# Two of three transposed K waves loaded as 16 rows of 131,072 columns, with score weights read at a step of 256 or 64 bytes

## The chip, the cores and the metric

The kernel runs on one core of one Trainium2 chip. The metric is the device time of one execution in microseconds (us). A short name is used throughout: TensorE is the matmul engine, and every matmul on it has its stationary operand, the weights, loaded by a weight load with its own record in the trace (PEld; the kernel before has 12,376 records of each). ScalarE (ACT), VectorE (DVE) and GpSimd (POOL) do the rest, and one queue on SyncE (SP) issues nearly all DMA (q1 of the page before: 291.99 of 294.14 MB).

Each set of experiments ran on one chip, with its own runs of the kernel before. Those runs had medians of 1054.96, 1054.72 and 1054.58 us for the three sets, so the sets can be compared to about half a microsecond.

## The reference, cut to what matters

There are two independent attention layers, A and B, of the same size. Each has 16 batches, 144 queries, 16 heads, 512 keys and a head width of 256, all in bf16.

```python
q = (x @ wq).reshape(16, 144, 16, 256).transpose(0, 2, 1, 3)
scores = einsum("bhqd,bhkd->bhqk", q, k_cache) * 256 ** -0.5
p = softmax(scores, axis=-1)
o = einsum("bhqk,bhkd->bhqd", p, v_cache)
out = o.transpose(0, 2, 1, 3).reshape(16, 144, 4096) @ wo
```

K and V of one head are 262 KB each, and there are 512 heads to go through (2 layers, 16 batches, 16 heads). One such head is called a unit. Several experiments below read wrong weights on purpose, and they passed all the same. Their times count, their results don't.

## The kernel before

The score matmuls of this kernel take K with the head width on the partitions (`kt_sb`), so K is transposed first. Units 0 to 47 have it done by TensorE. From unit 48 on, 29 "waves" of 16 units come in by a transposing DMA, into a ring of two waves. Every wave is one DMA of 4.19 MB:

```python
KW, KR = 16, 32                       # units in a wave, units in the ring
kt_sb = sb("kt_sb", [128, 8, KR * 128], BF16)
...
def t_load_k(W):
    ...
    src = ks[pr].rearrange("b h (p c) d -> (b h p) (c d)", c=4)[r0 * 128:(r0 + n) * 128, :]
    def e(q):
        return q.dma_start_transpose(kt_sb[:, :, c0:c0 + n * 128], src).then_inc(sems[sem], 16)
```

The source is read as 2048 rows of 1024 columns. After the transpose, the 128 weights of one score matmul lie next to each other in a partition. V comes by plain DMA, two units at a time, with one run of 2 KiB for each partition and unit. A key's place must agree between K and V: partition p holds keys 4p to 4p+3, as four chunks c.

```python
def v_source(t, G):
    ...
    return t[pr][b, h0:h0 + UV].rearrange("u (p c) d -> p u (c d)", p=128)

def t_s(U):                           # scores of one unit: 8 matmuls
    for k in range(2):
        for c in (2 * k, 2 * k + 1):
            for dc in range(2):
                t.matmul(s_ps[bank][:, (c % 2) * SQ:(c % 2 + 1) * SQ],
                         lhsT=kt_sb[:, 2 * c + dc, ko:ko + 128],
                         rhs=qt_sb[:, qsl, dc, :], start=(dc == 0), stop=(dc == 1))
        ...                           # exp on ScalarE into pt_sb
```

Besides these there are the query projection, the product with V (8 matmuls a unit), the sums of the exponentials on GpSimd, VectorE and TensorE, and the output projection. All of it is laid out ahead of time by a planner in the program. The planner issues each DMA by its own estimate of when the data is needed and of how long the queue is held; for a K wave of n units the estimate is `2.0 + 0.97 * n` us.

## Time and profile before

| | before |
|---|---|
| time, median of 2 runs | 1054.01 us (1053.67 to 1054.36) |
| span of the profiled run | 1051.6 us, mean granted clock 0.996 |
| TensorE busy | 1029.9 us, 98% |
| next busiest engine | ACT, 794.1 us, 76% |
| eight score matmuls, start to start of the next group | 0.50 us |
| time in which TensorE waited for a K wave | 6.9 us |

Two resources are near their end: TensorE, busy for 98% of the span, and the DMA queue, whose row of the forty slices stands at 9 up to the last two. The prediction below shows the lines for both. Two more rows of the page, from the list of the costliest groups, are wanted later. They are the score matmuls and their weight loads; the two numbers after the first bar are the busy time in us and the mean length of one record in ns, and behind the last bar stands the idle time of the engine before them with what ended most of it.

```profile
L1112 PE MATMUL s_ps<-qt_sb,kt_sb 128*128 128x144 bf16 x4096 | 341.3, 227 | 8.0 <-DMA kt_sb<-in_B_k_cache_dram 6.9
...
L1112 PEld LDWEIGHTS s_ps<-qt_sb,kt_sb 128*128 128x128 bf16 x4096 | 288.3, 98 | 60.0 <-issue 7.3
```

The mean records are 227 and 98 ns long, but one score matmul follows another after 62.5 ns. The records of successive matmuls thus overlap: each is 3.6 times as long as the distance to the next. What a matmul costs has to be read from start to start. And this is the DMA total of the page, with packets by size:

```profile
DMA packets 591748, 294.14 MB, mean 280 GB/s; under 512 B 502592, under 2 KB 516768, under 8 KB 591584
```

### The profile page before, as it was taken

How to read it: one execution, taken by the hardware profiler on the slowest of the kernel's cores; microseconds unless marked ns; L12 is line 12 of the kernel's file. 1: busy time of each engine (PE TensorE's matmuls, PEld its weight loads, DVE VectorE, ACT ScalarE, POOL GpSimd, SP SyncE). 2: the span in 40 equal slices, each digit the busy share in tenths (PEclk: the TensorE clock that was granted, in tenths of full speed). 3: DMA queues.
4: the chain of work that ended last, by engine and by line, in shares of the span. 5: the costliest groups of instructions: out<-in, count | busy, mean ns of one | idle time of the engine just before them, and what ended most of it. 6: DMA issues, size and time to landing. Idle time of an engine off the chain costs nothing.

```text
span 1051.6 us, 32329 instructions
## 1 busy us (share of the span) xinstructions
PE 1029.9 (98%) x12376; PEld 875.8 (83%) x12376; DVE 737.7 (70%) x2039; ACT 794.1 (76%) x2365; POOL 636.2 (61%) x1030
## 2 busy tenths in 40 slices
PE   7999999999999999999999799999999999999998
PEld 6999888888888888888888688888888888888885
DVE  5776676777776776676777567677776667777775
ACT  5877677777777787777877567787877777788785
POOL 3555556666666666666756456566666666666673
PEclk9999999999999999999999999999999999999999
DMA  9999999999999999999999999999999999999950
GB/s 291 363 341 340 263 306 266 288 288 293 290 300 284 285 237 257 302 290 297 265 288 340 268 276 300 295 272 300 282 269 269 299 258 305 302 271 257 289 187 14
DMA packets 591748, 294.14 MB, mean 280 GB/s; under 512 B 502592, under 2 KB 516768, under 8 KB 591584
## 3 DMA queue, kind: packets, MB, share of 16 engines
q1 hardware_dynamic: 591584, 291.99, 110.1%
q8 instruction: 99, 1.62, 0.6%
q14 instruction: 65, 0.53, 0.2%
HBM read 161.48 MB, written 4.13 MB: 157 GB/s over the span
## 4 chain that ended last, share of the span: by engine, by line
PE 90%; DMA 6%; SPq 1%; ACT 1%; DVE 1%; issue 0%; POOL 0%; ACTq 0%; DVEq 0%
PE s_ps L1112 23%; PE ot_ps L1168 23%; PE qp_ps L1081 22%; PE op_ps L1284 19%; DMA kt_sb<-in_B_k_cache_dram 2%; DMA kt_sb<-in_A_k_cache_dram 2%; PE ot_ps L1184 2%; DMA wq_sb<-in_A_wq_dram 1%; PE qp_ps L1032 1%; PE s_ps L1032 1%; PE qp_ps L1284 1%; ACT rinv_sb L1205 1%; DMA v_sb<-in_B_v_cache_dram 0%; SPq L1002 0%; ACT pt_sb L1122 0%
## 5 line engine op out<-in xcount | busy, mean ns | idle before, releaser
L1132 POOL TENSOR_TENSOR pp_sb<-pt_sb 128x288 f32<-128x288 bf16 x512 | 384.6, 751 | 320.1 <-ACT pt_sb L1122 305.4
L1122 ACT ACTIVATE pt_sb<-s_ps 128x288 bf16<-128x288 f32 x1024 | 364.6, 408 | 182.7 <-PE s_ps L1112 176.5
L1220 DVE TENSOR_TENSOR ring<-ot_ps,rinv_sb 128x288 bf16<-128x288 f32 (+2 forms) x640 | 241.8, 394 | 159.4 <-ACT rinv_sb L1205 155.0
L1112 PE MATMUL s_ps<-qt_sb,kt_sb 128*128 128x144 bf16 x4096 | 341.3, 227 | 8.0 <-DMA kt_sb<-in_B_k_cache_dram 6.9
L1168 PE MATMUL ot_ps<-pt_sb,v_sb 128*128 128x144 bf16 x4096 | 340.2, 226 | 0.3 <-DMA v_sb<-in_A_v_cache_dram 0.2
L1112 PEld LDWEIGHTS s_ps<-qt_sb,kt_sb 128*128 128x128 bf16 x4096 | 288.3, 98 | 60.0 <-issue 7.3
L1205 ACT ACTIVATE rinv_sb<-ln_sb 64x144 f32<-64x144 f32 x928 | 298.3, 321 | 24.2
L1081 PE MATMUL qp_ps<-xt_sb,wq_sb 128*128 128x288 bf16 (+1 forms) x2368 | 302.3, 271 | 2.2 <-DMA wq_sb<-in_A_wq_dram 1.2
L1284 PE MATMUL op_ps<-wo_sb,ring 128*128 128x448 bf16 x1120 | 285.5, 352 | 0.0
L1081 PEld LDWEIGHTS qp_ps<-xt_sb,wq_sb 128*128 128x128 bf16 x2368 | 212.7, 98 | 77.1 <-DVE qt_sb L1094 2.3
L1168 PEld LDWEIGHTS ot_ps<-pt_sb,v_sb 128*128 128x128 bf16 x4096 | 274.3, 98 | 1.2 <-DMA v_sb<-in_A_v_cache_dram 0.4
L1137 POOL TENSOR_TENSOR p_sb<-pp_sb 128x144 f32<-128x144 f32 x464 | 227.4, 490 | 74.2 <-DVE ps_sb L1146 9.4
L1235 DVE TENSOR_REDUCE run_sb<-ot_ps 128x1 bf16<-128x144 f32 x560 | 146.5, 304 | 76.7 <-ACT ln_sb L1192 42.6
L1146 DVE TENSOR_TENSOR ps_sb<-p_sb 64x144 bf16<-64x144 f32 x464 | 156.1, 336 | 45.8 <-POOL p_sb L1137 32.5
L1095 DVE CAST qt_sb<-qp_ps 128x576 bf16<-128x576 f32 x216 | 162.1, 750 | 14.0 <-PE qp_ps L1081 10.9
L1284 PEld LDWEIGHTS op_ps<-wo_sb,ring 128*128 128x128 bf16 x1120 | 93.7, 98 | 20.1
L1192 ACT ACTIVATE ln_sb<-ot_ps 128x144 f32<-128x144 f32 x232 | 67.9, 293 | 32.3 <-PE ot_ps L1184 24.5
L1184 PE MATMUL ot_ps<-ps_sb,ones 128*128 128x144 bf16 x280 | 63.3, 226 | 0.0
L1094 DVE CAST qt_sb<-qp_ps 128x288 bf16<-128x288 f32 x80 | 35.8, 447 | 2.8 <-PE qp_ps L1081 2.6
L1040 ACT ACTIVATE kt_sb<-qp_ps 128x512 bf16<-128x512 bf16 x48 | 28.9, 603 | 6.1 <-PE qp_ps L1032 6.1
L1137 POOL TENSOR_TENSOR ps_sb<-pp_sb 128x144 bf16<-128x144 f32 x48 | 23.5, 490 | 6.9 <-PE ot_ps L1184 0.3
L1184 PEld LDWEIGHTS ot_ps<-ps_sb,ones 128*128 128x128 bf16 x280 | 27.4, 98 | 0.0
(29 smaller groups left out, 154.5 us busy)
## 6 DMA issues: line engine op xcount, KB each, us to landing
v_sb<-in_A_v_cache_dram SPq DMA_DIRECT2D x128, 512.0 KB, 6.9
v_sb<-in_B_v_cache_dram SPq DMA_DIRECT2D x128, 512.0 KB, 7.0
v_sb<-in_A_k_cache_dram SPq DMA_DIRECT2D x22, 512.0 KB, 9.9
out_dram<-ost_sb SPq DMA_DIRECT2D x36, 112.0 KB, 6.1
wo_sb<-in_A_wo_dram SPq DMA_DIRECT2D x8, 448.0 KB, 8.5
wo_sb<-in_B_wo_dram SPq DMA_DIRECT2D x8, 448.0 KB, 8.7
wq_sb<-in_B_wq_dram SPq DMA_DIRECT2D x4, 768.0 KB, 9.3
wq_sb<-in_A_wq_dram SPq DMA_DIRECT2D x3, 768.0 KB, 9.2
```

The source lines that it names most:

```text
L1081: ins = t.matmul(acc, lhsT=wq_sb[:, kc, c0:c0 + 128], rhs=xt_sb[:, kc, xo:xe + 1:max(xe - xo, 1), :], start=(kc == 0), stop=(kc == 3))
L1095: return v.tensor_copy(qt_sb[:, a:b + 1:b - a, :, :], qp_ps[:, :, 0:2 * SQ].rearrange("p e (u q) -> p u e q", u=2))
L1112: ins = t.matmul(s_ps[bank][:, (c % 2) * SQ:(c % 2 + 1) * SQ], lhsT=kt_sb[:, 2 * c + dc, ko:ko + 128], rhs=qt_sb[:, qsl, dc, :], start=(dc ...
L1122: return a.activation(pt_sb[:, psl, 2 * k:2 * k + 2, :].rearrange("p b q -> p (b q)"), s_ps[bank][:, 0:2 * SQ], AF.Exp, scale=DH ** -0.5)
L1132: return g.tensor_tensor(pp_sb[:, :, :], pt_sb[:, psl, 0:2, :], pt_sb[:, psl, 2:4, :], op=ALU.add)
L1137: return g.tensor_tensor(dst, pp_sb[:, 0, :], pp_sb[:, 1, :], op=ALU.add)
L1146: return v.tensor_tensor(ps_sb[p0:p0 + 64, sl, :], p2_sb[0:64, :], p2_sb[64:128, :], op=ALU.add)
L1168: ins = t.matmul(ot_ps[ob][:, dc * SQ:(dc + 1) * SQ], lhsT=v_sb[:, vsl, j, c * DH + dc * 128:c * DH + (dc + 1) * 128], rhs=pt_sb[:, sl, c, ...
L1205: return a.activation(rinv_sb[p0:p0 + 64, sl, :], ln_sb[h0:h0 + 64, :], AF.Exp, scale=-1.0)
L1220: ins = v.tensor_tensor(ring[:, 2 * h:2 * h + 2, r0:r0 + q1 - q0], ot_ps[ob][:, 0:2 * SQ].rearrange("p (c q) -> p c q", c=2)[:, :, q0:q1], ...
L1235: return v.tensor_reduce(run_sb[:, k, j:j + 1], ot_ps[ob][:, 2 * SQ:3 * SQ], axis=AX.X, op=op)
L1284: ins = t.matmul(acc[0:m, 0:D], lhsT=ring[:, c, col0:col0 + m], rhs=wo_sb[:, c, :], start=(c == op_first), stop=(c == op_last))
```

## The change

The intent is to load K in longer rows. Of every three waves one stays as it was (form 0). In the other two the source is read as 16 rows, one for each head, of 131,072 columns, so that each row is 256 KiB in one piece. The price is that the transposed data lies otherwise in the ring: element k of head u is followed by element k of head u+1. The 128 weights of one matmul are then no longer neighbours.

- Form 1 keeps the key order 4p + c. It reads every 128th element, a step of 256 bytes.
- Form 2 takes the key order 128c + p. It reads every 32nd element, a step of 64 bytes. V has to follow that order, so its runs shrink from 2 KiB to 512 bytes.

```diff
-        kt_sb = sb("kt_sb", [128, 8, KR * 128], BF16)
+        kt_sb = sb("kt_sb", [128, KR // KW, KW * 1024], BF16)
...
             src = ks[pr].rearrange("b h (p c) d -> (b h p) (c d)", c=4)[r0 * 128:(r0 + n) * 128, :]
+            if k_form(u0):
+                src = ks[pr].rearrange("b h k d -> (b h) (k d)")[r0:r0 + n, :]
...
+                dst = kt_sb[:, u0 % KR // KW, :]
+                if k_form(u0):
+                    dst = dst.rearrange("p (k u) -> p k u", u=KW)
+                else:
+                    dst = dst.rearrange("p (c n) -> p c n", c=8)
+                return q.dma_start_transpose(dst, src).then_inc(sems[sem], 16)
...
+        def k_form(U):
+            return 0 if U < P0 else U // KW % 3
+
+        def k_weights(U, c, dc):
+            ring = kt_sb[:, U % KR // KW, :]
+            f = k_form(U)
+            if f == 0:
+                return ring.rearrange("p (c n) -> p c n", c=8)[:, 2 * c + dc, U % KW * 128:U % KW * 128 + 128]
+            ring = ring.rearrange("p (k e u) -> p k e u", u=KW, e=2)[:, :, dc, U % KW]
+            return ring[:, c::4] if f == 1 else ring[:, c * 128:(c + 1) * 128]
...
+            if k_form(UV * G) == 2:
+                return t[pr][b, h0:h0 + UV].rearrange("u (c p) d -> p u c d", p=128)
...
-                                           lhsT=kt_sb[:, 2 * c + dc, ko:ko + 128],
+                                           lhsT=k_weights(U, c, dc),
```

Left out are the V destination with the same dimensions and the same ring indexing in the copy of TensorE's transposes. No instruction is added on any engine, and their order stays.

More of the change, by code (lines that the diff above doesn't have):

```diff
@@ L985, in t_load_k @@
             src = ks[pr].rearrange("b h (p c) d -> (b h p) (c d)", c=4)[r0 * 128:(r0 + n) * 128, :]
+            if k_form(u0):
+                src = ks[pr].rearrange("b h k d -> (b h) (k d)")[r0:r0 + n, :]
             def e(q):
-                return q.dma_start_transpose(kt_sb[:, :, c0:c0 + n * 128], src).then_inc(sems[sem], 16)
-            S.add(SP, e, writes=[(("kt", u % KR), u) for u in range(u0, u1)], dma_sem=sem, name="k%d.%d" % (W, n))
+                dst = kt_sb[:, u0 % KR // KW, :]
[4 more added lines that the diff above has]
+                return q.dma_start_transpose(dst, src).then_inc(sems[sem], 16)
+            S.add(SP, e, writes=[(("kt", u % KR), u) for u in range(u0, u1)], dma_sem=sem, name="k%d.%d" % (W, n))
+        def k_form(U):
[7 more added lines that the diff above has]
+            return ring[:, c::4] if f == 1 else ring[:, c * 128:(c + 1) * 128]
         def v_source(t, G):
@@ L1001, in e @@
             def e(q):
-                return q.dma_start(v_sb[:, sl, :, :], src).then_inc(sems["v%d" % sl], 16)
+                dst = v_sb[:, sl, :, :]
+                if k_form(UV * G) == 2:
+                    dst = dst.rearrange("p u (c d) -> p u c d", c=4)
+                return q.dma_start(dst, src).then_inc(sems["v%d" % sl], 16)
             S.add(SP, e, writes=[(("v", sl), ("v", G))], dma_sem="v%d" % sl, name="v%d" % G)
@@ L1037, in ev @@
             def ev(g):
-                dst = kt_sb[:, 4 * k:4 * k + 4, ko:ko + 128]
+                dst = kt_sb[:, U % KR // KW, :].rearrange("p (c n) -> p c n", c=8)[:, 4 * k:4 * k + 4, U % KW * 128:U % KW * 128 + 128]
                 src = tr_ps[k][:, 0:512].rearrange("p (c q) -> p c q", c=4)
```

## The prediction

> **What bounds the kernel now.** I read first the page's busy shares and its forty slices, then the groups by cost, then the order of matmuls, the weight loads of the score line, the DMA queue in order of time, and last the stretches between.
>
> ```profile
> PE 1029.9 (98%) x12376; PEld 875.8 (83%) x12376; DVE 737.7 (70%) x2039; ACT 794.1 (76%) x2365; POOL 636.2 (61%) x1030
> ...
> DMA  9999999999999999999999999999999999999950
> ...
> PE s_ps L1112 <- DMA kt_sb<-in_B_k_cache_dram: 6.9, 1, 6.9
> ```
>
> TensorE is busy for 1029.9 of 1051.6 us, so all of its idle time is 21.7 us: about 6 in the first 10 us, 5.6 in the last 32, and 6.9 in one wait for a K wave (third line, from the list of waits; it is the only one that counts). No other engine is over 76%. The DMA row, though, is as full as TensorE's. So there are two resources near their end. Which of them has how much room decides the case.
>
> TensorE first. A matmul's record overlaps its neighbours', so I take start to start from the order of time:
>
> ```profile
> 20.42 0.39 PE L1032 MATMUL s_ps<-qt_sb,v_sb 128*128 128x128 bf16 x4
> 20.64 0.66 PE L1081 MATMUL qp_ps<-xt_sb,wq_sb 128*128 128x144 bf16 x8
> 21.14 0.66 PE L1112 MATMUL s_ps<-qt_sb,kt_sb 128*128 128x144 bf16 x8
> 21.64 0.39 PE L1032 MATMUL qp_ps<-qt_sb,v_sb 128*128 128x128 bf16 x4
> ```
>
> Eight score matmuls take 21.64 - 21.14 = 0.50 us, 62.5 ns each; four transposes with 128 moving columns take 0.22 us, 55 ns each. Each of these has its own weight load, all from adjacent columns. So a contiguous load needs at most 55 ns and lies wholly beside the matmul before it. Nothing in this trace loads weights with a step, so the disputed cost isn't there to be read. What is there is one clue:
>
> ```profile
> L1112 PEld LDWEIGHTS s_ps<-qt_sb,kt_sb x16: 95/98/98, 300.1 to 301.7; 128*128 128x128 bf16 x16
> ...
> L1112 PEld LDWEIGHTS s_ps<-qt_sb,kt_sb x8: 104/147/147, 602.0 to 602.7; 128*128 128x128 bf16 x8
> ```
>
> (min/median/max ns of two windows.) Right after the 6.9 us wait TensorE runs slow: eight score matmuls begin within 0.91 us, not 0.50, and the load's record grows by 49 ns. If the clock halved there, as 0.91/0.50 suggests, the part that scales with the clock is about 49 ns at full speed[...]. I rest on this with care, since the page says that ends are modelled.
>
> DMA second.
>
> ```profile
> 245.17 19.03 SPq L988 DMA_TRANSPOSE kt_sb<-in_A_k_cache_dram  x1
> 264.24 0.58 SPq L1313 DMA_DIRECT2D out_dram<-ost_sb  x1
> 264.87 7.16 SPq L1002 DMA_DIRECT2D v_sb<-in_A_v_cache_dram  x7
> ...
> 248.00:263.00 15.00, 15.00 (x176) 12.47 (x174) 10.76 (x29) 11.18 (x35) 9.78 (x16) 1.00 1.30 226
> 267.00:273.00 6.00, 6.00 (x75) 5.07 (x73) 3.81 (x10) 4.75 (x15) 3.59 (x6) 1.00 1.01 385
> ```
>
> A wave of 16 heads is one transpose of 4.19 MB. It holds the queue for 19 us and runs at 226 GB/s (last column of the windows), where plain V loads run at 385. K waves are issued 30 to 31 us apart here (214.6, 245.2): 19 for K, 8 V loads of 0.52 MB at 385 GB/s are 11 more. The queue is nearly full, but TensorE still sets the pace.
>
> [...]
>
> **The change, part by part.** Waves begin at unit 48, so there are 29; those with number 4, 7, ... 31 (10) take the 256-byte step, 5, 8, ... 29 (9) the 64-byte step, and 10 stay. 19 waves x 16 units x 8 = 2432 of 4096 score matmuls get stepped weights. The order of instructions on every engine is the old one; no matmul, exponential or sum is added. The ring has the same size, and 16 units are freed at the same place.
>
> K transposes: 19 move the same 4.19 MB from 16 contiguous rows of 256 KiB instead of 2048 rows of 2 KiB. [...] This is work beside TensorE: it relieves the queue and shortens nothing, except that the wave waited for at 602 us (still an old one, but behind two new ones in the queue) arrives earlier. That returns 6.9 us and the slow-clock stretch behind it, about 2 us: -9.
>
> V loads of the 9 waves with the 64-byte step: 72 loads in runs of 512 bytes instead of 2 KiB. Even 20% more than 1.4 us (0.52 MB at 385 GB/s) is 0.3 x 8 = 2 us a wave, and the faster K pays for it: 0.
>
> Weight loads: my main line is that [...] the slot of a score matmul is set by the load[...]. The first load of eight runs beside the last matmul of another group, mostly 288 or 448 columns wide (0.98 us/8 = 123 ns, 0.38/2 = 190 ns), so seven of eight pay[...] x 304 units = 95 us, all on the path since TensorE has no slack.
>
> Sum: 1054 + 95 - 9 = 1140 us.
>
> **Rivals.**
> A, the load stays hidden: [...] only the -9 is left: 1045 us. [...]
> [...]
> C, the transpose becomes the bound[...]. A wave has 30.5 us of TensorE work and 11 of V loads, so a transpose over 19.5 us begins to cost its excess; at 25 us, 19 x 5.5 = 105 us. If loads also slow down, TensorE takes 16 x 0.31 = 5 us longer a changed wave and hides that much. The only 16-row transposes of the trace are two of 384 columns, 12 KB, landing after 2.9 to 3.4 us, too small to tell. I hold it for 1 in 6.
> D, a real gain: TensorE's idle total is 21.7 us and a dozen of it is start and end, so over 2% (21 us) is out of reach unless matmuls get faster.
>
> **Range and chances.** I give some 0.55 to a visible cost of the step [...], and of the rest one part in eight to C. Hidden loads end at 1043 to 1056; a cost between a third and one and a half times the 95 us ends at 1075 to 1190, with something of C on top to 1230. The range has to hold both peaks: 1043 to 1230. The point lies at the upper peak, though nearly two in five of the chances are at the lower. Faster 0.02, same 0.38, slower 0.60.
>
> **What would show it.** [...] eight take 0.81 to 0.86 us instead of 0.50, and the old-form waves keep 0.50: this is the step to look at first, and the prediction is wrong if they keep 0.50 everywhere. Weight-load records at the score line split into 98 ns and about 150. Both steps cost alike[...]. Changed transposes [...] pass 226 GB/s; over 20 us means C. The 6.9 us wait is gone. DMA row: down from 9 in changed waves. Other groups on TensorE keep their counts and durations.

## More of the kernel before

The inputs are small: x and K have a deviation of 0.1, and wq one of 0.1 divided by the root of 448. A score therefore has a deviation of about 0.001, the softmax is all but uniform, and the comparison with the reference did not notice wrong score weights.

## The result, and the profile after

The changed kernel took 1110.97 us, the median of two runs (1110.66 to 1111.27). The ratio to the kernel before is 1.054, with a 95% interval of 1.0495 to 1.0586. Ratios here and below are the mean time of one kernel's fast runs over that of the other's of the same rounds, so they are not quite the ratio of the medians that are quoted. The profiled run had a span of 1108.9 us and again a granted clock of 0.996, so the clock has no part in it.

These are the busy shares, the DMA row of the forty slices and the DMA total of the page after:

```profile
PE 1087.9 (98%) x12376; PEld 940.7 (85%) x12376; DVE 794.9 (72%) x2039; ACT 845.8 (76%) x2365; POOL 702.5 (63%) x1030
...
DMA  9999999999999999999999999999999999999930
...
DMA packets 647043, 294.13 MB, mean 265 GB/s; under 512 B 502592, under 2 KB 590496, under 8 KB 646880
```

TensorE is busy for 1087.9 us, 58.0 more than before, with the same 12,376 matmuls. Its idle time is 21.0 us, where it was 21.7. So all of the added 57.3 us of span is TensorE work that got slower, and none of it is waiting. The DMA row stayed at 9 up to the last two slices. The 55,295 added packets are the shorter V runs: 72 loads of 128 partitions, 2 units and 3 more runs each make 55,296.

These are the same groups as those shown of before:

```profile
L1135 PE MATMUL s_ps<-qt_sb,kt_sb 128*128 128x144 bf16 x4096 | 398.1, 240 | 6.4 <-DMA kt_sb<-in_B_k_cache_dram 3.8
...
L1135 PEld LDWEIGHTS s_ps<-qt_sb,kt_sb 128*128 128x128 bf16 x4096 | 366.9, 150 | 51.1 <-DVE qt_sb L1118 12.3
```

The score matmuls are busy for 56.8 us more (341.3 to 398.1). That is the whole difference, on one line of the program. Their mean weight-load record went from 98 to 150 ns, and the K wait from 6.9 to 3.8 us.

To see which waves pay, here is TensorE in order of time, in three stretches: a 256-byte wave, a 64-byte wave and a wave of the old form. The columns are start and length in us; each pair is the score group of a unit and the group after it.

```profile
151.94 0.98 PE L1135 MATMUL s_ps<-qt_sb,kt_sb 128*128 128x144 bf16 x8
152.75 0.66 PE L1191 MATMUL ot_ps<-pt_sb,v_sb 128*128 128x144 bf16 x8
...
196.37 0.67 PE L1135 MATMUL s_ps<-qt_sb,kt_sb 128*128 128x144 bf16 x8
196.88 0.66 PE L1191 MATMUL ot_ps<-pt_sb,v_sb 128*128 128x144 bf16 x8
...
220.32 0.66 PE L1135 MATMUL s_ps<-qt_sb,kt_sb 128*128 128x144 bf16 x8
220.82 0.66 PE L1191 MATMUL ot_ps<-pt_sb,v_sb 128*128 128x144 bf16 x8
```

From start to start, eight score matmuls take 152.75 - 151.94 = 0.81 us with the 256-byte step, 0.51 with the 64-byte step, and 0.50 in the old form. Over all waves the means of the first two are 0.840 and 0.519 us; of the third the median is 0.500, as before. With 160 units of the first kind and 144 of the second this makes 160 x 0.340 + 144 x 0.019 = 54.4 + 2.7 = 57.1 us. The shorter K wait takes back 3.1 us, which would leave 54. The whole trace, summed from the start of each matmul to that of the next without idle time, closes the account: 56.7 us more in the score matmuls, 1.3 us more in all other groups, and only 1.2 us less idle time between matmuls, because small waits elsewhere ate up most of what the K wait gave back.

The weight loads of the same three waves, with minimum, median and maximum record in ns:

```profile
L1135 PEld LDWEIGHTS s_ps<-qt_sb,kt_sb x92: 207/220/258, 154.8 to 179.9; 128*128 128x128 bf16 x92
...
L1135 PEld LDWEIGHTS s_ps<-qt_sb,kt_sb x116: 137/144/222, 185.8 to 214.4; 128*128 128x128 bf16 x116
...
L1135 PEld LDWEIGHTS s_ps<-qt_sb,kt_sb x128: 95/98/98, 220.1 to 249.8; 128*128 128x128 bf16 x128
```

The record grows by 46 ns with the 64-byte step, but the slot of a matmul grows by 2.4 ns only (0.019 us over eight). The record of a load is no measure of what it costs.

The transposes are seen in the DMA queue in order of time, and in a window of whole-queue work inside the same transpose. The last column of the window is GB/s.

```profile
219.57 16.45 SPq L995 DMA_TRANSPOSE kt_sb<-in_A_k_cache_dram  x1
...
221.00:234.00 13.00, 13.00 (x152) 10.85 (x150) 9.34 (x28) 10.50 (x32) 8.19 (x14) 1.00 1.27 254
```

This transpose of the new kind moves 254 GB/s. One window in each of the 29 transposes of before gives 220 to 287.

These are groups of other engines, first in the window of the 256-byte wave and then in that of the old form. The number wanted is the second one after the bar, the mean ns of one instruction.

```profile
L1155 POOL TENSOR_TENSOR pp_sb<-pt_sb 128x288 f32<-128x288 bf16 x13 | 14.2, 1092 | 5.2 <-ACT pt_sb L1145 4.9
L1228 ACT ACTIVATE rinv_sb<-ln_sb 64x144 f32<-64x144 f32 x26 | 11.5, 442 | 0.7
L1145 ACT ACTIVATE pt_sb<-s_ps 128x288 bf16<-128x288 f32 x26 | 9.9, 409 | 3.8 <-PE s_ps L1135 3.6
L1169 DVE TENSOR_TENSOR ps_sb<-p_sb 64x144 bf16<-64x144 f32 x13 | 8.9, 683 | 0.4
...
L1155 POOL TENSOR_TENSOR pp_sb<-pt_sb 128x288 f32<-128x288 bf16 x15 | 11.3, 753 | 8.4 <-ACT pt_sb L1145 8.2
L1145 ACT ACTIVATE pt_sb<-s_ps 128x288 bf16<-128x288 f32 x30 | 10.7, 408 | 4.3 <-PE s_ps L1135 4.2
L1228 ACT ACTIVATE rinv_sb<-ln_sb 64x144 f32<-64x144 f32 x31 | 10.0, 322 | 0.8
L1169 DVE TENSOR_TENSOR ps_sb<-p_sb 64x144 bf16<-64x144 f32 x15 | 4.8, 320 | 0.5
```

While weights are read at 256 bytes, GpSimd's sum goes from 753 to 1092 ns and ScalarE's reciprocal from 322 to 442. VectorE's sum of two halves goes from 320 to 683. All three read tiles that the program puts in SBUF (their names end in `_sb`), as it does `kt_sb`. ScalarE's exponential reads `s_ps`, a tile in PSUM that the score matmuls write, and it is at 409 against 408. In the other nine 256-byte waves the picture is the same: their means are 804 to 1210, 370 to 508 and 475 to 716 ns for the three, and 411 to 430 for the exponential. VectorE's reduction that reads PSUM stays near its 303 ns (295 to 313). Whether GpSimd and VectorE also hold each other up in part, these runs don't tell.

### The profile page after: what moved, and what is told of

Same layout as the page of the kernel before. It is cut to its first block, busy times and chain, and to the rows that moved or that the text cites. A ratio compares the mean times of both kernels' runs of the same rounds, so it can differ in the third digit from the quotient of the medians.

```text
span 1108.9 us, 32329 instructions
## 1 busy us (share of the span) xinstructions
PE 1087.9 (98%) x12376; PEld 940.7 (85%) x12376; DVE 794.9 (72%) x2039; ACT 845.8 (76%) x2365; POOL 702.5 (63%) x1030
## 4 chain that ended last, share of the span: by engine, by line
PE 90%; DMA 3%; ACT 3%; DVE 2%; SPq 1%; issue 1%; POOL 0%; ACTq 0%; DVEq 0%
PE s_ps L1135 26%; PE ot_ps L1191 21%; PE qp_ps L1104 21%; PE op_ps L1307 18%; DMA kt_sb<-in_B_k_cache_dram 2%; PE ot_ps L1207 2%; ACT rinv_sb L1228 1%; DMA wq_sb<-in_A_wq_dram 1%; PE s_ps L1055 1%; PE qp_ps L1055 1%; DVE ring L1243 1%; ACT pt_sb L1145 1%; PE qp_ps L1307 1%; DVE qt_sb L1118 0%; ACT ln_sb L1215 0%
## 5 line engine op out<-in xcount | busy, mean ns | idle before, releaser
L1155 POOL TENSOR_TENSOR pp_sb<-pt_sb 128x288 f32<-128x288 bf16 x512 | 425.8, 832 | 305.1 <-ACT pt_sb L1145 288.3
L1145 ACT ACTIVATE pt_sb<-s_ps 128x288 bf16<-128x288 f32 x1024 | 375.1, 411 | 186.1 <-PE s_ps L1135 179.6
L1135 PEld LDWEIGHTS s_ps<-qt_sb,kt_sb 128*128 128x128 bf16 x4096 | 366.9, 150 | 51.1 <-DVE qt_sb L1118 12.3
L1135 PE MATMUL s_ps<-qt_sb,kt_sb 128*128 128x144 bf16 x4096 | 398.1, 240 | 6.4 <-DMA kt_sb<-in_B_k_cache_dram 3.8
L1243 DVE TENSOR_TENSOR ring<-ot_ps,rinv_sb 128x288 bf16<-128x288 f32 (+2 forms) x640 | 264.9, 431 | 157.9 <-ACT rinv_sb L1228 146.6
L1228 ACT ACTIVATE rinv_sb<-ln_sb 64x144 f32<-64x144 f32 x928 | 332.8, 359 | 24.2
L1160 POOL TENSOR_TENSOR p_sb<-pp_sb 128x144 f32<-128x144 f32 x464 | 252.5, 544 | 80.1 <-DVE ps_sb L1169 20.5
L1191 PEld LDWEIGHTS ot_ps<-pt_sb,v_sb 128*128 128x128 bf16 x4096 | 281.6, 100 | 0.7 <-DMA v_sb<-in_A_v_cache_dram 0.2
L1169 DVE TENSOR_TENSOR ps_sb<-p_sb 64x144 bf16<-64x144 f32 x464 | 193.2, 416 | 48.6 <-POOL p_sb L1160 35.3
L1215 ACT ACTIVATE ln_sb<-ot_ps 128x144 f32<-128x144 f32 x232 | 74.5, 321 | 34.2 <-PE ot_ps L1207 28.3
```

The lines of the kernel that those rows point to most:

```text
L1135: ins = t.matmul(s_ps[bank][:, (c % 2) * SQ:(c % 2 + 1) * SQ], lhsT=k_weights(U, c, dc), rhs=qt_sb[:, qsl, dc, :], start=(dc == 0), stop=( ...
L1145: return a.activation(pt_sb[:, psl, 2 * k:2 * k + 2, :].rearrange("p b q -> p (b q)"), s_ps[bank][:, 0:2 * SQ], AF.Exp, scale=DH ** -0.5)
L1155: return g.tensor_tensor(pp_sb[:, :, :], pt_sb[:, psl, 0:2, :], pt_sb[:, psl, 2:4, :], op=ALU.add)
L1160: return g.tensor_tensor(dst, pp_sb[:, 0, :], pp_sb[:, 1, :], op=ALU.add)
L1169: return v.tensor_tensor(ps_sb[p0:p0 + 64, sl, :], p2_sb[0:64, :], p2_sb[64:128, :], op=ALU.add)
L1191: ins = t.matmul(ot_ps[ob][:, dc * SQ:(dc + 1) * SQ], lhsT=v_sb[:, vsl, j, c * DH + dc * 128:c * DH + (dc + 1) * 128], rhs=pt_sb[:, sl, c, ...
```

## The experiments

There were two theories at the start. The first says that the stepped weight load is the cost, and that some property of the step decides how large it is: whether there is a step at all, whether it is 16 bytes or more, how far apart the elements are, or whether the step is a power of two. The expectation of `sweep` calls the last three line, distance and bank theory; the names stand for guesses of mine, and no run shows what lies behind them. The rival says that the cost comes from DMA: the 16-row transposes, or the 512-byte V runs.

### Stepped reads alone, and loads alone

`step_only` keeps the stepped reads and loads K and V as before. Its scores are wrong.

```diff
-            if k_form(u0):              # twice, source and destination of K
+            if False:
-            if k_form(UV * G) == 2:     # twice, source and destination of V
+            if False:
```

> Old transposes and old V layout in all waves; only the score weights are read with steps of 256 bytes (10 waves) and 64 bytes (9 waves), so the result is wrong on purpose. Theory S (the step of the weight load is the whole cost): 1105 to 1116 us, score blocks of eight 0.79 to 0.90 us in the 256-byte waves and 0.52 in the 64-byte waves, as in the changed kernel. Rival D (the new transposes or the new V layout disturb TensorE's reads): 1050 to 1056 us and 0.50 us blocks.

It took 1107.42 us (1105.43 to 1107.71), a ratio of 1.0491 [1.0475, 1.0507]. These are its weight loads in a 256-byte and a 64-byte wave:

```profile
L1135 PEld LDWEIGHTS s_ps<-qt_sb,kt_sb x88: 205/224/251, 155.4 to 179.1; 128*128 128x128 bf16 x88
...
L1135 PEld LDWEIGHTS s_ps<-qt_sb,kt_sb x120: 136/143/246, 186.5 to 215.6; 128*128 128x128 bf16 x120
```

The records are those of the changed kernel, and so are the blocks of eight matmuls, 0.838 and 0.520 us. The reads alone bring 52.5 us of the 57. The slowing of the other engines is there too (GpSimd 1081, ScalarE 460, VectorE 680 ns), although no DMA was changed. The transposes of the 19 waves in question, old form here, held the queue for 18.6 us on average, as short as the new ones in the changed kernel (18.6) and shorter than in the kernel before (19.4). The wait for a K wave is gone altogether.

`form_only` is the complement: the new loads of K and V, and weights read as neighbours. Its scores are wrong too.

```diff
-            if f == 0:                  # in k_weights
+            if True:
```

> New transposes of 16 rows and new V layout, but the score weights are read from adjacent columns (wrong result on purpose). Theory S: the cost is gone, 1043 to 1054 us; if the new transposes relieve the queue, under 1050 and the wait for a K wave is under 3.8 us. Rival D: 1105 to 1116 us.

It took 1072.88 us (1072.44 to 1074.46), 1.0174 [1.016, 1.0188]. The median score block of every wave is back at 0.50 us. So the loads cost 18 us by themselves, which I had not allowed for. The waits show where: 8.1 us for a K wave, 6.6 for query weights, and some for V. But 52.5 and 18 are more than 57: in the changed kernel most of the load cost is hidden.

### Which load is it: K or V?

`k16_only` takes the new transposes alone, with weights read as neighbours (wrong) and V as before.

```diff
-            if f == 0:                  # in k_weights
+            if True:
-            if k_form(UV * G) == 2:     # twice, V
+            if False:
```

> Only the transposes of 19 waves take 16 rows of 131072 columns; V loads as before, weights from adjacent columns (wrong result on purpose). Theory V: 1045 to 1056 us, with K transposes no shorter than before by more than 1 us. Theory K: 1068 to 1076 us. My prediction's step [...]: under 1048 us.

It took 1054.49 us (1054.26 to 1056.6), 1.0005 [0.9993, 1.0017]. Two windows in the transfers of its new transposes, a 256-byte and a 64-byte wave, GB/s in the last column:

```profile
222.00:236.00 14.00, 14.00 (x164) 11.58 (x162) 10.35 (x27) 10.45 (x33) 8.92 (x16) 1.00 1.27 263
...
248.00:262.00 14.00, 14.00 (x163) 11.53 (x161) 9.94 (x26) 10.73 (x33) 9.01 (x15) 1.00 1.29 227
```

In the same two windows the kernel before moved 259 and 222 GB/s, for the same two waves. Over all 19 waves the new transposes held the queue for 20.2 us on average, the old ones 19.4. Rows of 256 KiB are thus moved no faster than rows of 2 KiB, and hardly slower. The time is the same, and the wait for K stays at 6.9 us. What the change was made for brings nothing.

`v_only` takes the 512-byte V runs of the nine form-2 waves alone (K loads and weights as before, so the keys of K and V do not match).

```diff
-            if k_form(u0):              # twice, K
+            if False:
-            if f == 0:                  # in k_weights
+            if True:
```

> Only the V loads of 9 waves take the new layout (four runs of 512 bytes instead of one of 2 KiB); transposes and weight reads as before (wrong result on purpose). Theory V (the 18 us of form_only are the short runs of V): 1068 to 1076 us. Theory K (they are the 16-row transposes): 1052 to 1057 us. Half each: about 1063.

It took 1071.76 us (1069.65 to 1075.78), 1.0167 [1.0146, 1.0187]. These are the largest of its waits for DMA (us in all, number of waits, longest):

```profile
PE s_ps L1135 <- DMA kt_sb<-in_B_k_cache_dram: 9.0, 1, 9.0
...
PE qp_ps L1104 <- DMA wq_sb<-in_B_wq_dram: 8.3, 1, 8.3
...
PE ot_ps L1191 <- DMA v_sb<-in_B_v_cache_dram: 2.0, 1, 2.0
```

That is 17.0 us, nearly all of what `form_only` lost (17.9). The V runs hold the queue longer (277 to 297 GB/s in `all_64` below, against 385 to 392 before), and other loads behind them come late.

### One form alone, or one form everywhere

`only_256` gives the second form back to the old one, so ten waves have the 256-byte step and V is as before. Its scores are right.

```diff
-            return 0 if U < P0 else U // KW % 3
+            return 0 if U < P0 or U // KW % 3 != 1 else 1
```

> Right result: of the change only the 10 waves with the 256-byte step (16-row transposes, V loads in the old layout). Step cost alone, 160 units x 0.33 us = 53 us, less part of the K wait: 1100 to 1110 us.

It took 1103.9 us (1103.34 to 1104.87), 1.0474 [1.0458, 1.0489]. That is 49.3 us for 160 units, or 0.31 us a unit, with K waits down to 0.6 us. The estimate from the blocks, 54.4 less the 6.3 us of wait saved, is 48.1.

`only_64` is the same with `!= 2 else 2`: nine waves have the 64-byte step and 512-byte V runs.

> Right result: of the change only the 9 waves with the 64-byte step and their V loads in runs of 512 bytes. If the V loads cost what v_only showed when no wave is slowed by its weights, 17 us, and the weights 144 x 0.02 = 3 us: 1070 to 1078 us. Together with only_256 that adds to some 72 us, more than the 57 of the whole change; if instead the V loads cost only 4 us of their own, 1056 to 1062 us and the two parts add up.

It took 1072.72 us (1071.51 to 1072.97), 1.0176 [1.0161, 1.019]. That is 18.1 us, as much as `v_only` within the intervals, with K waits of 8.3 and 6.5 us for query weights. The 64-byte step itself is nearly free; the V layout that it needs is not.

`all_64` uses the second form for all 29 waves, with right results.

```diff
-            return 0 if U < P0 else U // KW % 3
+            return 0 if U < P0 else 2
```

> All 29 waves take the 64-byte form (right result). Theory S with the block times of the changed kernel (0.52 against 0.50 us): 464 units x 0.02 to 0.025 us = 9 to 12 us more, less a few us of K wait: 1055 to 1066 us. A theory in which any step over 16 bytes costs the same and the 64-byte waves were spared by chance: over 1150 us.

It took 1130.4 us (1124.98 to 1132.75), 1.0706 [1.0681, 1.073], with a granted clock of 0.973. My expectation missed it: I had it between 1055 and 1066. The score blocks are where I expected them, at 0.51 to 0.52 us, but TensorE's waits for DMA rose from 15 to 65 us. The rest of the 76 us is slower matmuls at the lower clock: summed from start to start, 12.8 us in the score matmuls and 13 in all other groups. Two windows with almost nothing but V loads, and the largest waits:

```profile
248.00:258.00 10.00, 10.00 (x120) 8.46 (x118) 7.40 (x20) 8.43 (x27) 6.16 (x11) 1.00 1.08 277
...
285.00:295.00 10.00, 10.00 (x115) 8.47 (x113) 6.62 (x18) 7.55 (x23) 6.20 (x11) 1.00 1.07 290
```

```profile
PE ot_ps L1191 <- DMA v_sb<-in_B_v_cache_dram: 19.1, 8, 4.0
PE ot_ps L1191 <- DMA v_sb<-in_A_v_cache_dram: 16.6, 4, 6.8
...
PE s_ps L1135 <- DMA kt_sb<-in_B_k_cache_dram: 11.8, 4, 5.7
```

V loads in runs of 512 bytes move 277 to 297 GB/s, where runs of 2 KiB move 385 to 392. A load of 0.524 MB then takes about 1.84 us instead of 1.36, or 8 x 0.48 = 3.8 us more queue time a wave. With this in 29 waves TensorE waits 65 us for DMA, where it waited 15.

### What it is about the step

`sweep` gives each of the 29 waves another step, with old loads (wrong scores). Successive loads of a unit begin 2 bytes apart.

```diff
+        STEPS = (1, 2, 4, 8, 12, 16, 20, 24, 28, 32, 34, 36, 40, 48, 56, 64, 65, 72, 80, 88, 96, 104, 112, 120, 124, 126, 127, 128, 1)
...
+            if U >= P0:                 # in k_weights
+                st = STEPS[U // KW - P0 // KW]
+                j = U % KW * 8 + 2 * c + dc
+                return ring[:, j:j + 127 * st + 1:st]
```

> Old transposes; each of the 29 waves reads its score weights with its own step: 2, 4, 8, 16, 24, 32, 40, 48, 56, 64, 68, 72, 80, 96, 112, 128, 130, 144, 160, 176, 192, 208, 224, 240, 248, 252, 254, 256, 2 bytes (wrong result on purpose). Line theory [...]: records of the load jump at 16 bytes and stay flat above. Bank theory [...]: 256 bytes near 220 ns, 64 near 144, 128 between the two, and steps that are no power of two (112, 144, 176, 208, 240, 252) well under 220 ns although they are as large. Distance theory (cost grows with the step): 240 to 254 bytes near 220 ns, rising evenly from 64.

`sweep2` varies the distance between the beginnings of successive loads as well. PAT is a list of 29 pairs of step and distance.

```diff
+            if U >= P0:                 # in k_weights
+                st, dl = PAT[U // KW - P0 // KW]
+                j = (U % KW * 8 + (2 * c + dc) * dl) % 128
+                return ring[:, j:j + 127 * st + 1:st]
```

> As sweep, with the successive loads of a unit offset by a chosen distance: 256-byte step with 0, 2, 16, 32, 64, 128 bytes between loads, 128 with 0, 2, 16, 32, 64, 160 with 0, 2, 16, 32, 64, 64 with 2, 32, 64, then 48, 120, 152, 168, 156, 164, 124, 132, 250, 2 bytes with 16 (wrong result on purpose). If one load alone is slow, blocks of a step are alike at every offset: 256 bytes 0.95, 128 bytes 0.70, 160 bytes 0.63 us. [...] If multiples of 32 bytes were what costs, 152 and 168 are at 0.51 beside 160 at 0.63.

Both are single looks (1074.3 and 1118.1 us); what counts in them is the score block of each wave, a median over its units. The first table is from `sweep`, with successive loads 2 bytes apart.

| step, bytes | eight matmuls, us | load record, ns |
|---|---|---|
| 2, 4 | 0.50 | 98 |
| 8 | 0.50 | 114 |
| 16, 24, 32, 56, 64 | 0.51 to 0.52 | 143 to 144 |
| 48 | 0.55 | 157 |
| 128 | 0.70 | 195 |
| 130 | 0.51 | 143 |
| 160 | 0.63 | 177 |
| 192, 208, 224, 240 | 0.50 to 0.51 | 140 to 143 |
| 248 | 0.56 | 156 |
| 254 | 0.50 | 137 |
| 256 | 0.95 | 254 |

The steps left out lie between 0.50 and 0.54 us. The second table is from `sweep2`, by the distance of successive loads.

| step | 0 bytes apart | 2 | 16 and more |
|---|---|---|---|
| 256 | 0.98 | 0.945 | 0.82 to 0.835 |
| 128 | 0.70 | 0.70 to 0.705 | 0.675 |
| 160 | 0.63 | 0.63 to 0.64 | 0.63 to 0.64 |

In the 256-byte waves of the changed kernel successive loads begin 32 bytes apart, so its block of 0.84 us is that of the last column.

The steps of 48 and 160 bytes give 0.55 and 0.63 again at other distances. Steps of 164 and 168 bytes give 0.62 and 0.59, and 120 gives 0.515. Some of the weight loads behind the first table, at 128, 160, 192, 248 and 256 bytes:

```profile
L1141 PEld LDWEIGHTS s_ps<-qt_sb,kt_sb x112: 167/195/216, 609.1 to 638.8; 128*128 128x128 bf16 x112
...
L1141 PEld LDWEIGHTS s_ps<-qt_sb,kt_sb x112: 158/177/183, 708.0 to 735.5; 128*128 128x128 bf16 x112
...
L1141 PEld LDWEIGHTS s_ps<-qt_sb,kt_sb x115: 134/141/153, 770.4 to 797.2; 128*128 128x128 bf16 x115
...
L1141 PEld LDWEIGHTS s_ps<-qt_sb,kt_sb x113: 146/156/173, 898.9 to 926.7; 128*128 128x128 bf16 x113
...
L1141 PEld LDWEIGHTS s_ps<-qt_sb,kt_sb x120: 208/254/309, 994.4 to 1029.3; 128*128 128x128 bf16 x120
```

Four things follow. A step as such costs almost nothing: from 4 to 64 bytes, apart from 48, the block stays within 0.02 us of the contiguous one. Up to 16 bytes the record grows and the block hardly: the record is 98 ns at 4 bytes, 114 at 8, 143 to 144 at 16 and 137 to 143 at the larger steps of the table that cost little, while the block is at 0.50 to 0.52 us. Distance does not decide either, since 192 to 240 and 254 bytes (0.50 to 0.51 us) are as cheap as 16. What costs are particular steps: 256 most (0.95 us), then 128 (0.70), then those around 160 (0.63), with small humps at 48, 248 and beside 128 (0.54 to 0.56 us at 124, 132 and 152 to 156). Why these, no run shows; 64 bytes at 0.52 and the hump at 160 do not fit a plain power-of-two rule. The exact rule stays open. The other engines slow down at 256 bytes, not at 128 or 160: in `sweep2` GpSimd's sum took 857 to 1193 ns in the six 256-byte waves and 734 to 782 in the ten at 128 and 160, VectorE's sum of two halves 428 to 813 against 305 to 348, and ScalarE's reciprocal 407 to 484 in five of the six (321 in the first) against 323 to 325.

### Can the wait of before be had in another way?

The K wait of 6.9 us was the largest single wait left in the kernel before, so two runs tried to take it by the planner. `took` lets the planner expect longer K holds and thus issue them earlier:

```diff
-                load(..., 2.0 + 0.97 * (u1 - u0), t_load_k, W)
+                load(..., 2.0 + 1.2 * (u1 - u0), t_load_k, W)
```

> The kernel before, with the K transpose planned at 1.2 instead of 0.97 us a unit, which moves K loads earlier in the queue. If the 6.9 us wait for a K wave is all that can be had: 1043 to 1048 us; if the queue only moves its lateness to V loads: 1052 to 1060 us.

It took 1068.39 us (1067.47 to 1070.09), 1.0133 [1.0116, 1.015]. The K waits got worse, 15.3 us in two and 2.6 in a third. With the queue as full as it is, planning more time for each wave shifts the rest; that is my reading of the waits.

`hold` changes the constant with which the planner decides whether a K wave or another load goes first.

```diff
-    MARGIN, HOLD = 1.0, 1.0
+    MARGIN, HOLD = 1.0, -1.0
```

> The kernel before with the planner's HOLD at -1 instead of 1, which puts two K waves at the start of the second problem two and one V loads earlier. If the 6.9 us wait can be had without making V late: 1044 to 1050 us; if the queue has no room: 1052 to 1060 us.

It took 1054.33 us (1051.49 to 1054.73), 0.9996 [0.9984, 1.0007]: nothing. The K wait is gone, but TensorE waits 5.9 us for query weights of the second layer in its place: the queue only moves its lateness. No version that beats both kernels was found.

## Why the prediction was right or wrong

The outcome, slower by over 2%, was the likeliest of the three, and 1110.97 us lies in the range. The predicted point was 29 us too high, and a range 187 us wide left room for that. The mechanism named, a weight load that sets the slot of a score matmul, is the one that acts, as `step_only` shows: stepped reads with the old loads bring 52.5 of 57 us. Its details were half wrong.

**The term that was mis-sized.** The prediction put the stepped loads at 95 us for 304 units, so at 0.31 us a unit for both steps. That size was my estimate: the trace of before has no load with a step to read it from. It measured 57. For the 256-byte waves the size was right: 0.340 us a unit against 0.31, so 54.4 us against 50. For the 144 units with 64 bytes it was wrong: 0.019 us a unit, so 2.7 us against 45. The 95 were thus 38 us too high in all; the 9 us that the prediction took off, and that did not come in the sum, hid part of this and left the miss of 29. That part was luck. Within a 256-byte block seven of the eight intervals grow by 44 ns on average, and the first, which the prediction left out, grows by 30. The prediction named the test itself: "Both steps cost alike". They don't.

**The reason given for it.** If both steps cost alike, it is the step as such that costs. The prediction had no trace for this, and it falls: weights at 4 and at 64 bytes both run at 0.50 to 0.52 us. Nor is there one slot that a costly step gives: it is 105 ns in the 256-byte waves of the change, 88 at 128 bytes, 79 at 160, and 119 at 256 bytes with loads 2 bytes apart. The load records, too, split into 98, 143 and 220 ns and not into 98 and about 150. The clue in the trace was the load record's growth by 49 ns in the stretch after the long wait, where the granted clock is 0.50 (602 to 606 us); it was read as the part of the load that scales with the clock. The sweep shows that records may grow by 45 ns with a slot that grows by 2.

**The K transposes.** They were to be faster than the old ones, so that a new transpose "relieves the queue". That was my estimate, and it did not come: the windows show 227 to 263 GB/s in `k16_only` and 230 to 272 in the 19 new transposes of the changed kernel, where the old ones had 220 to 287. The shorter holds of the queue in the changed kernel, 16.45 us where 19.03 was shown before, would have looked like a success of the new form. They are there in `step_only` with old transposes too (18.6 us on average in both), so they do not come from the form; that they come from the slack of a slower TensorE is my reading, and no run shows it by itself.

**The wait.** "-9" was 3.1 for the wait itself. `k16_only` leaves the wait at 6.9, so the new transposes did not return it. It shrinks where TensorE is slower: to 0.6 us in `only_256`, and to nothing in `step_only` with its old transposes. (The idle time at the end, "5.6 in the last 32", reads 5.1 in the trace; nothing rests on it.)

**The V loads.** "The faster K pays for it: 0" was wrong in its reason and near in its effect. K was not faster, and the V runs cost 17 us alone (`v_only`). The allowance of 20%, 2 us a wave, was too small: 277 to 297 GB/s mean 3.8 us. Over nine waves that is some 35 us of queue time. In the changed kernel the ten 256-byte waves make TensorE some 54 us slower, which is room for the queue to catch up. The whole change added 57.0 us to its kernel before and `step_only` 52.5 to the one beside it, so all the new loads added only 4.5 us here. That hiding is inferred from the sum of the parts: 49.3 and 18.1 make 67.4, and together they measured 57.0.

**The rivals.** A, hidden loads, is what the 64-byte step does (0.51 to 0.52 us a block). C, the transpose as the bound, does not occur, as `k16_only` shows (1054.49 us); its sign, holds over 20 us, is seen in some changed waves, but in the kernel before as well (up to 26.4). A DMA bound came from V instead, in `all_64` (65 us of waits for DMA). D, no gain over 2%, held. Other TensorE groups kept their counts, as predicted, but the DMA row did not fall below 9.

## What to carry to other kernels

Read the cost of a weight load from the starts of successive matmuls, not from its record (at 64 bytes 46 ns more in the record were 2.4 in the slot). When a layout makes a stationary operand strided, try the very step on the chip: here 4 to 64 bytes (48 less so) and most others were nearly free (0.50 to 0.52 us for eight matmuls), and 256, 128 and about 160 bytes were not (0.95, 0.70 and 0.63). Count the layout's price on the other operand too; here the cheap step forced short V runs, which cost 17 us through the full queue, where the step took 2.7 us from TensorE.
